# Attention and two feed-forward layers on one core: head 0's decay row, the first zeros, and when two weight conversions run

## The chip, the core and the metric

The kernel runs on one core of a Trainium2 chip. Five engines work side by side, each through its own instructions in order: TensorE (matrix products, PE in the profile), VectorE (DVE), ScalarE (ACT), GpSimd (POOL) and SyncE (SP), which here issues every DMA. The metric is the device time in microseconds, the median over several runs. The order in which each engine gets its instructions is made by a planner when the kernel is built: it takes the program's order as priority and a model of times as its guide, so a line that stands later in the program can come earlier on its engine when its data is there.

## The reference

Three parts follow each other. The first is causal attention with a decay, over 4 batches of 8 heads, 576 positions of 64:

```python
scores = scale * np.matmul(q, k.transpose(0, 1, 3, 2))
cum = np.cumsum(np.maximum(s, 0.0), axis=-1)
bias = -(cum[:, :, :, None] - cum[:, :, None, :])
scores = np.where(causal, -1000000000.0, scores + np.minimum(bias, 0.0))
attn = softmax(scores)
x = attn @ v                      # 2304 tokens x 512 after a transpose
```

The second is `((x @ w1) * (x @ w2)) @ w3 @ w_out` with a width of 1024. The third is `h = x @ w_in`, then `h * softmax(h)`, a layer norm with the gain `g_ln`, and a last product with `w_out`.

## The kernel before

**Attention.** For each head, `qk_part` computes the scores of the causal part in five query tiles (`QT`) as matrix products, `softmax_tile` masks a tile and takes its maximum on VectorE (L195) and its exponential and sum on ScalarE (L199). `normalise` scales the rows by the reciprocal sum on both engines (L227, L228, L235, L237). `tr_part` transposes the probabilities on TensorE (L256) and copies them out of the accumulators (`evict`). `av_parts` multiplies pairs of heads with their values (L284).

The decay is put into the product itself: the operands of a head have 128 rows, 64 with data (64 to 127), and in the lower half a row of ones and a row with the running sum `cum`, the other way round for the keys, and zeros elsewhere. For the first eight heads (`NQ`) these operands stand in plain float32: `QN[h % 3]` and `KN[h % 3]`, three pairs of them. The first two pairs are tiles of their own, the third is `qk3`, which takes over the slot of `s_sb`. Their zeros are memsets, their constant rows come from `const_rows` (ScalarE, L490), and `load_aug` sends the row of `cum` by two small DMAs, row 32 of Q (L155) and row 0 of K (L156). From head 8 on the operands are split into two parts (`split_qk`, with a subtraction on GpSimd at L99 and a copy by DMA at L168).

`cum` is made once: a load of `s`, a scaling (L500) and a scan (L501) on VectorE, and a copy of its last 64 columns to the front (L502). The masks are `wmask`, zero until GpSimd puts the diagonal in after the scan (L517), and `lmask`, a zeroed tile (L499) that then takes two pieces of `wmask`. Before any data is there, TensorE multiplies a zeroed tile with itself eight times (L472).

**The weights.** They arrive as 64-bit floats, 512 KB at a time, in a `stage` tile with two buffers (L394). A conversion (`split_w` with `to_f32`) takes six instructions: ScalarE at L349, VectorE at L355, L356 and L360, then ScalarE (L94) and VectorE (L99) write the two parts of the weight. `pump(n)` in a step loads what fits into the buffers, issues n conversions, each held behind the latest first-tile softmax of a head (`behind`), and loads again. A buffer is free after its conversion.

**Steps.** The loop at L555 runs steps. Step h below 8 computes the scores of head h and transposes head h - 2. Steps 8 and 9 have no scores: they transpose heads 6 and 7 and finish the value products. Step 10 begins with head 8, and from there each step also runs units of `a = x @ w1`, `b = x @ w2` (`ab_unit`, L312; L324 and L332 take them out), as many as `NF` says. `PUMP` says how many conversions a step issues: one each in steps 3, 5 and 6, then two in steps 10 to 15 and one in step 16, sixteen in all for `w1` and `w2`. The units need their weights from step 10 on. After the last head the remaining units, the product of `w3` and `w_out` (L637), the product x (L720), the third part and the output (L854) follow.

The order around the change on SP: the load of `s`, heads 0 and 1, the rows of heads 0 and 1, head 2 (L136, L137) and its row, the two stores of the sums (L513, L516), the gain (L533).

Of the kernel before, what the change touches and what calls it, by code (L numbers as in the profile page):

```python
# [12 lines left out]
AF = mybir.ActivationFunctionType  # L13
# [13 lines left out]
def tile_attention_moe(  # L27
# [15 lines left out]
    nc = tc.nc  # L43
    B, H, D, _, S = qkT.shape
# [7 lines left out]
    HS = S // 2  # L52
# [33 lines left out]
    def smalltile(name):  # L86
        return PSP[1].tile([128, 512], F32, tag="B", name=name)

    def flat(ap):
        return ap.rearrange("p a b -> p (a b)")  # L90
# [25 lines left out]
    lmask = at.tile([128, S], F32, name="lmask")  # L116
# [5 lines left out]
    QN = [t[:, 0] for t in QKN]  # L122
    KN = [t[:, 1] for t in QKN]
# [9 lines left out]
    def load_head(h):  # L133
        b, hh = divmod(h, H)
        if h < NQ:
            nc.sync.dma_start(out=QN[h % 3][64:128], in_=qkT[b, hh, :, 0])  # L136
            after[0] = nc.sync.dma_start(out=KN[h % 3][64:128], in_=qkT[b, hh, :, 1])  # L137
            return
        qk2 = at.tile([128, 2, S], F32, tag="qk2", bufs=2, name="qk2")
        after[0] = nc.sync.dma_start(  # L140
            out=qk2[64:128].rearrange("p a s -> p (a s)"), in_=qkT[b, hh].rearrange("d a s -> d (a s)"),
        )
        raw_t[h] = qk2[64:128]
# [9 lines left out]
    def load_aug(h, src):  # L153
        if h < NQ:
            nc.sync.dma_start(out=QN[h % 3][32:33], in_=src[:, 64:])  # L155
            nc.sync.dma_start(out=KN[h % 3][0:1], in_=src[:, 0:S])  # L156
            return
        nc.sync.dma_start(out=QK[h % 2][32:34, 0].bitcast(F32), in_=src[:, 64:].bitcast(F32))
        nc.sync.dma_start(out=QK[h % 2][0:2, 3].bitcast(F32), in_=src[:, 0:S].bitcast(F32))
# [242 lines left out]
    def pump(n):  # L402
        for _ in range(n):
            load_jobs()
            if loaded:
                raw, conv = loaded.pop(0)

                with ExitStack() as order:
                    for ins in behind:
                        order.enter_context(tc.issue_after(ins))  # L410
                    conv(raw)
        load_jobs()
# [55 lines left out]
    zz = r0.tile([128, HS], F32, tag="a_sb", bufs=2, name="zz")  # L468
    nc.vector.memset(zz, 0.0)
    zp = smalltile("zp")  # L470
    for i in range(8):
        nc.tensor.matmul(zp[:, 0:HS], zz[:, 0:128], zz, start=True, stop=True)  # L472
    s_sb = at.tile([NH, 2, S], F32, tag="qk2", bufs=2, name="s_sb")[:, 0]
    nc.sync.dma_start(out=s_sb, in_=s.rearrange("b h t -> (b h) t"))
# [3 lines left out]
    cum = flat(at.tile([NH, 2, S], F32, tag="qk2", bufs=2, name="cum"))[:, 0:S + 64]  # L478
# [9 lines left out]
    def const_rows(q_, k_):  # L488
        for dst, src, value in ((q_[0:2], zz[0:2], 1.0), (k_[32:34], zz[32:34], -1.0)):
            nc.scalar.activation(  # L490
                out=dst.rearrange("p (a s) -> p a s", a=2), in_=src[:, None, :].broadcast_to((2, 2, HS)),
                func=AF.Copy, scale=0.0, bias=value,
            )

    for i, eng in enumerate((nc.gpsimd, nc.vector)):
        eng.memset(QN[i][0:64], 0.0)
        eng.memset(KN[i][0:64], 0.0)
        const_rows(QN[i], KN[i])
    nc.gpsimd.memset(lmask, 0.0)  # L499
    nc.vector.tensor_scalar(out=s_sb, in0=s_sb, scalar1=0.0, scalar2=1.0 / SCALE, op0=ALU.max, op1=ALU.mult)  # L500
    nc.vector.tensor_tensor_scan(out=cum[:, 64:], data0=s_sb, data1=wmask[0:NH], initial=0.0, op0=ALU.add, op1=ALU.add)  # L501
    nc.vector.tensor_copy(out=cum[:, 0:64], in_=cum[:, S:])  # L502
    for i in range(2):
        load_aug(i, cum[i:i + 1])

    qk3 = at.tile([128, 2, S], F32, tag="qk2", bufs=2, name="qk3")
    QN.append(qk3[:, 0])
    KN.append(qk3[:, 1])
    nc.vector.memset(qk3[0:64], 0.0)
    const_rows(QN[2], KN[2])  # L510
    load_head(2)
    load_aug(2, cum[2:3])
    nc.sync.dma_start(out=cumf_scr, in_=cum)  # L513
    hi(CK[:, 0], cum, nc.vector)
    lo(CK[:, 1], cum, CK[:, 0])
# [2 lines left out]
        out=wmask[:, S - 128:S], in_=wmask[:, S - 128:S], pattern=[[-1, 128]],  # L518
# [5 lines left out]
    behind_scan.__enter__()  # L524
    for st in STAT:
        nc.gpsimd.memset(st, 1.0)
    for t in PT:
        for j in (2, 3, 1):
            nc.gpsimd.memset(t[64:128, KO[j]:KO[j] + 64], 0.0)
    for t in VT:  # L530
        nc.gpsimd.memset(t[0:64, 4], 0.0)
    behind_scan.__exit__(None, None, None)
    nc.sync.dma_start(out=gln, in_=g_ln.rearrange("(k p) -> p k", p=128))  # L533

    for f in range(KF):
# [12 lines left out]
    steps += [(h if h < NH else None, h - 2 if h >= H + 2 else None) for h in range(H, NH + 2)]  # L548
    NF = {10: 3, 11: 0, 12: 3, 13: 0, 14: 3, 15: 2, 16: 2, 17: 0, 18: 1, 19: 1, 20: 1, 21: 2, 22: 2, 23: 2, 24: 2, 25: 2, 26: 2, 27: 2, 28: 2, 29: 2, 30: 2, 31: 2, 32: 2, 33: 2, 34: 3, 35: 3}
    PD, FS = 10, 0.5  # L550
    PUMP = {3: 1, 5: 1, 6: 1, 10: 2, 11: 2, 12: 2, 13: 2, 14: 2, 15: 2, 16: 1}
    PUMP.update((i, 1 if i < 30 else 2) for i in range(22, 34))
    fill = []
    late = []
    for st, (h, ph) in enumerate(steps):  # L555
# [18 lines left out]
        if st > 1:  # L574
            pump(PUMP.get(st, 0))
        if h is not None:
# [461 lines left out]
```

## Time and profile before

| what | value |
|---|---|
| median of 3 runs | 723.62 us (723.31 to 725.47) |
| the profiled execution | 724.28 us, span 722.2 us |
| TensorE busy | 706.0 us (98%) |
| VectorE busy | 509.3 us (71%) |
| ScalarE busy | 467.8 us (65%) |
| GpSimd busy | 94.1 us (13%) |

The span runs from the first instruction to the last; the execution's own time has some 2 us more around it. The shares are means over stages with different limits. Records of TensorE are modelled at their ends, so that its busy share says little in a stretch where it has much waiting; the waits and the busy times of the other engines in that stretch say more. A row of the timeline merges neighbours of one kind: its second number is then the time from the first one's start to the last one's end, with their number behind the x. In brackets stands the engine's idle time before it and what ended it.

### The profile page before, as it was taken

Reading aid. Unit: us, or ns where it says so; the run is one execution under the profiler, and the core shown is the slowest. Engines: PE = TensorE matmul, PEld = TensorE weight load, DVE = VectorE, ACT = ScalarE, POOL = GpSimd, SP = SyncE. Lnnn points to the kernel's source line nnn. Section 1 sums busy time; section 2 is a strip of 40 time slices with the busy share of each in tenths; the row PEclk is TensorE's granted clock in tenths of the full one; section 3 lists DMA queues with packets and bytes.
Section 4 is the critical chain, followed back from the end, with each engine's and each line's share of the span. In section 5 each row is a group of like instructions: output and inputs, shape, how many; then the busy total and the mean of one; then the engine's idle time right before and its main releaser. Section 6 shows DMA issues by size and latency. Waiting matters only on the chain.

```text
span 722.2 us, 12948 instructions
## 1 busy us (share of the span) xinstructions
PE 706.0 (98%) x4642; PEld 630.9 (87%) x4642; DVE 509.3 (71%) x1252; ACT 467.8 (65%) x978; POOL 94.1 (13%) x88
## 2 busy tenths in 40 slices
PE   9989898999999999999999999999999999999998
PEld 6669888889999999999998889988888988888887
DVE  7997989997878888722787985656747366563751
ACT  7997878798866777822544665656647465564742
POOL 2051322143221221000000000001000000000000
PEclk9999999999999999999999999999999999999999
DMA  4654645454476665514565964242334142303211
GB/s 118 191 138 123 175 154 162 154 147 123 138 231 187 193 183 178 183 63 150 181 209 171 331 207 113 66 110 68 82 87 103 44 131 74 89 13 76 59 45 44
DMA packets 79972, 95.53 MB, mean 132 GB/s; under 512 B 41434, under 2 KB 52954, under 8 KB 79908
## 3 DMA queue, kind: packets, MB, share of 16 engines
q1 hardware_dynamic: 79908, 94.71, 45.2%
q8 instruction: 36, 0.59, 0.3%
q14 instruction: 28, 0.23, 0.1%
HBM read 59.04 MB, written 20.17 MB: 110 GB/s over the span
## 4 chain that ended last, share of the span: by engine, by line
PE 76%; DVE 12%; DMA 4%; ACT 4%; issue 2%; POOL 0%; DVEq 0%; ACTq 0%
PE a L312 12%; PE o L854 12%; PE b L312 12%; PE x L720 11%; PE m L637 6%; PE av L284 4%; PE tr L256 4%; PE hX L752 4%; PE hZ L752 3%; DMA turned<-half 3%; DVE P L195 2%; PE sc L186 2%; PE sc L187 2%; ACT P L199 1%; DMA stage<-in_w_dram 1%
## 5 line engine op out<-in xcount | busy, mean ns | idle before, releaser
L199 ACT ACTIVATE P<-P,STAT 128x576 f32<-128x576 f32 (+4 forms) x160 | 88.2, 553 | 18.7 <-DVE STAT L195 18.1
L99 POOL TENSOR_TENSOR QK<-qk,QK 64x1152 fp32r<-64x1152 f32 x24 | 66.6, 2776 | 169.4 <-ACT QK L94 169.3
L720 PE MATMUL x<-gh,ML 128*128 128x256 f32 x288 | 80.3, 279 | 0.0
L720 PE MATMUL x<-gl,MH 128*128 128x256 f32 x288 | 80.1, 279 | 0.0
L720 PE MATMUL x<-gh,MH 128*128 128x256 f32 x288 | 80.0, 279 | 0.0
L312 PE MATMUL a<-xT0h,W 128*128 128x288 f32 x256 | 58.6, 303 | 3.6 <-ACT PT L94 3.3
L312 PE MATMUL b<-xT0h,W 128*128 128x288 f32 x256 | 57.5, 298 | 1.9 <-DVE g_sb L332 1.7
L854 PE MATMUL o<-OH,lh 128*128 128x512 f32 (+1 forms) x152 | 57.7, 379 | 0.2 <-DVE ll L99 0.2
L816 DVE COPY lt<-turned 128x2048 uint16<-128x2048 uint16 x16 | 21.5, 1344 | 51.1 <-DMA turned<-half 51.1
L854 PE MATMUL o<-OL,lh 128*128 128x512 f32 (+1 forms) x152 | 57.5, 378 | 0.0
L854 PE MATMUL o<-OH,ll 128*128 128x512 f32 (+1 forms) x152 | 57.5, 378 | 0.0
L256 PE MATMUL tr<-ident,P 128*128 128x128 f32 x416 | 54.2, 274 | 3.1 <-DVE PT L96 1.0
L312 PE MATMUL a<-xT1h,W 128*128 128x288 f32 x256 | 57.2, 298 | 0.0
L312 PE MATMUL b<-xT1h,W 128*128 128x288 f32 x256 | 56.5, 294 | 0.0
L720 PEld LDWEIGHTS x<-gl,MH 128*128 128x128 f32 x288 | 54.1, 188 | 1.3
L720 PEld LDWEIGHTS x<-gh,MH 128*128 128x128 f32 x288 | 54.1, 188 | 1.0
L720 PEld LDWEIGHTS x<-gh,ML 128*128 128x128 f32 x288 | 54.1, 188 | 0.8
L96 DVE COPY PT<-tr 64x192 f32<-64x192 f32 (+2 forms) x96 | 40.4, 432 | 17.8 <-PE tr L256 17.8
L349 ACT ACTIVATE stage<-stage 128x512 f32<-128x512 f32 x56 | 37.0, 679 | 24.2 <-DMA stage<-in_w_dram 22.0
L256 PEld LDWEIGHTS tr<-ident,P 128*128 128x128 f32 x416 | 47.1, 141 | 5.8 <-DVE PT L96 1.4
L332 DVE TENSOR_TENSOR g_sb<-b,a_sb 128x288 f32<-128x288 f32 x64 | 28.7, 449 | 30.0 <-PE b L312 20.0
L324 ACT ACTIVATE a_sb<-a 128x288 f32<-128x288 f32 x64 | 25.5, 401 | 36.3 <-PE a L312 36.2
(192 smaller groups left out, 1988.0 us busy)
## 6 DMA issues: line engine op xcount, KB each, us to landing
stage<-in_w_dram SPq DMA_DIRECT2D x32, 512.0 KB
g_scr<-g_sb SPq DMA_DIRECT2D x32, 288.0 KB
stage<-in_wo_dram SPq DMA_DIRECT2D x16, 512.0 KB
qk<-in_qk_dram SPq DMA_DIRECT2D x24, 288.0 KB
QK<-QK SPq DMA_DIRECT2D x24, 288.0 KB
gl<-g_scr SPq DMA_DIRECT2D x24, 256.0 KB
wf<-wf_scr SPq DMA_DIRECT2D x22, 256.0 KB
out_dram<-o SPq DMA_DIRECT2D x17, 256.0 KB
```

Of the source, the lines that this page charges most:

```text
L96: eng.tensor_copy(out=dst, in_=src)
L99: last_lo[0] = eng.tensor_tensor(out=dst, in0=src, in1=hi_.bitcast(F32), op=ALU.subtract).ins
L199: ex = nc.scalar.activation(out=dst, in_=dst, func=AF.Exp, bias=st[0:rows, ti:ti + 1], scale=-1.0, accum_out=st[0:rows, 5 + ti:6 + ti],)
L256: last_tr[0] = nc.tensor.transpose(ps[:, 128 * n:128 * n + 128], pt[:, o:o + 128], ident)
L284: nc.tensor.matmul(st["ps"][64 * e:64 * e + 64, 448 + c0:448 + c1], vr[:, j, e], PT[(2 * p + e) % 4][:, o + c0:o + c1], **kw,)
L312: nc.tensor.matmul(ps, w_[:, c, fs], x_[:, c, sl], start=(c == 0 and w_ is WH and x_ is XH), stop=(c == KC - 1 and w_ is WL),)
L332: ab_last[1] = nc.vector.tensor_tensor(out=g[:, sl], in0=ps, in1=st["a"], op=ALU.mult).ins
L349: nc.scalar.activation(out=high.bitcast(F32), in_=high.bitcast(F32), func=AF.Copy, scale=2.0 ** -112)
L637: nc.tensor.matmul(ps, w_[:, k % 4], o_[:, k], start=(k == 0 and w_ is H3 and o_ is WOH), stop=(k == KF - 1 and w_ is L3),)
L720: last = nc.tensor.matmul(ps[:, a], w_[:, k, m * 128:m * 128 + 128], g_[:, k % 2], start=(k == 0 and w_ is MH and g_ is GH), stop=(k == KF ...
L752: last_h[0] = nc.tensor.matmul(ps, x_[:, k], w_[:, k], start=first and k == 0 and x_ is XH and w_ is WH, stop=k == 1 and x_ is XL, skip_gr ...
L854: last = nc.tensor.matmul(ps, l_[:, k], w_[:, k, c0:c1], start=(k == 0 and l_ is LH and w_ is OH), stop=(k == KF - 1 and l_ is LL),)
```

## The change

Head 0's row of `cum` is copied by VectorE instead of sent by two DMAs: the Q row straight behind the scan, the K row behind the copy of the last 64 columns. The eight zero products become four. The zeros of `lmask` are written by ScalarE from the zeroed tile instead of by GpSimd, and the zeros of `qk3` by GpSimd instead of VectorE, at a later place: behind the diagonal and the small memsets of the statistics. The constant rows and the row of head 2 move behind those zeros. Of the three conversions of steps 3, 5 and 6 one stays in step 6; two now stand in steps 8 and 9.

```diff
-    for i in range(8):
+    for i in range(4):
         nc.tensor.matmul(zp[:, 0:HS], zz[:, 0:128], zz, start=True, stop=True)
...
-    nc.gpsimd.memset(lmask, 0.0)
+    nc.scalar.activation(
+        out=lmask.rearrange("p (a s) -> p a s", a=2), in_=zz[:, None, :].broadcast_to((128, 2, HS)), func=AF.Copy,
+    )
     nc.vector.tensor_scalar(out=s_sb, in0=s_sb, scalar1=0.0, scalar2=1.0 / SCALE, op0=ALU.max, op1=ALU.mult)
     nc.vector.tensor_tensor_scan(out=cum[:, 64:], data0=s_sb, data1=wmask[0:NH], initial=0.0, op0=ALU.add, op1=ALU.add)
+    nc.vector.tensor_copy(out=QN[0][32:33], in_=cum[0:1, 64:])
     nc.vector.tensor_copy(out=cum[:, 0:64], in_=cum[:, S:])
-    for i in range(2):
-        load_aug(i, cum[i:i + 1])
+    nc.vector.tensor_copy(out=KN[0][0:1], in_=cum[0:1, 0:S])
+    load_aug(1, cum[1:2])
...
-    nc.vector.memset(qk3[0:64], 0.0)
-    const_rows(QN[2], KN[2])
     load_head(2)
-    load_aug(2, cum[2:3])
...
     for st in STAT:
         nc.gpsimd.memset(st, 1.0)
+    nc.gpsimd.memset(qk3[0:64], 0.0)
...
     behind_scan.__exit__(None, None, None)
+    const_rows(QN[2], KN[2])
+    load_aug(2, cum[2:3])
...
-    PUMP = {3: 1, 5: 1, 6: 1, 10: 2, 11: 2, 12: 2, 13: 2, 14: 2, 15: 2, 16: 1}
+    PUMP = {6: 1, 8: 1, 9: 1, 10: 2, 11: 2, 12: 2, 13: 2, 14: 2, 15: 2, 16: 1}
```

## Rows read from the trace of the kernel before

**Rows 1.** TensorE's waits from 175 us on: total us, times, longest.
```profile
PE hX L752 <- ACT so L758: 0.5, 1, 0.5
```

**Rows 2.** Windows: start:end, length, busy us by engine, clock, DMA share, GB/s.
```profile
10.00:52.00 42.00, 38.09 (x223) 28.69 (x222) 39.41 (x146) 41.90 (x121) 8.49 (x10) 1.00 0.61 165
...
49.00:62.00 13.00, 11.97 (x88) 9.59 (x90) 9.71 (x28) 10.22 (x28) 3.40 (x3) 1.00 0.41 111
```

**Rows 3.** Timeline of the start: start us, us, engine, line, what, [idle before].
```profile
3.75 1.34 DVE L501 TENSOR_TENSOR_SCAN cum<-s_sb,wmask 32x576 f32<-32x576 f32 x1
...
5.12 0.18 DVE L502 COPY cum<-cum 32x64 f32<-32x64 f32 x1
...
5.88 0.53 SPq L156 DMA_DIRECT2D QKN<-cum  x1
...
6.44 0.47 DVE L96 CAST CK<-cum 32x640 fp32r<-32x640 f32 x1
...
9.02 0.76 DVE L195 CUSTOM_DVE_ANT_0 P<-sc,lmask 128x576 f32<-128x576 f32 x1 [1.26 <-PE sc L178]
...
9.82 0.77 ACT L199 ACTIVATE P<-P,STAT 128x576 f32<-128x576 f32 x1 [1.90 <-DVE STAT L195]
```

**Rows 4.** Timeline of TensorE: zero products left at three times, first scores.
```profile
1.25 6.57 PE L472 MATMUL zp<-zz 128*128 128x288 f32 x16 [1.25 <-DVE zz L469]
...
4.29 3.53 PE L472 MATMUL zp<-zz 128*128 128x288 f32 x10
...
6.44 1.38 PE L472 MATMUL zp<-zz 128*128 128x288 f32 x5
...
7.65 0.45 PE L178 MATMUL sc<-QKN 128*128 128x288 f32 x1
```

**Rows 5.** Windows of one us on TensorE: busy us, granted clock.
```profile
118.00:119.00 1.00, 0.00 (x0) 0.91 0.56 129
...
122.00:123.00 1.00, 1.00 (x8) 0.89 0.37 60
```

**Rows 6.** Timeline of the start: what stands around the edits costed at nothing.
```profile
5.49 1.02 DVE L509 MEMSET qk<- 64x1152 f32 x1 [0.19 <-issue]
...
5.50 0.40 ACT L94 ACTIVATE lmask<-wmask 128x64 f32<-128x64 f32 x2 [0.94 <-POOL wmask L517]
...
5.72 1.43 POOL L529 MEMSET PT<- 64x64 f32 x12
...
6.55 1.38 ACT L490 ACTIVATE qk<-zz 2x576 f32<-2x576 f32 x2 [0.65 <-DVE qk L509]
...
9.63 0.59 SPq L156 DMA_DIRECT2D qk<-cum  x1
...
13.15 1.32 PEld L178 LDWEIGHTS sc<-qk 128*128 128x128 f32 x6
```

**Rows 7.** Windows of the staged weights' instructions alone: VectorE's, ScalarE's busy us.
```profile
20.00:36.00 16.00, 4.63 (x8) 2.75 (x4) 1.00 0.65 183
```

**Rows 8.** Timeline of the fifth stage load, step 10's conversions and the next loads.
```profile
48.27 0.36 SPq L394 DMA_DIRECT2D stage<-in_w_dram  x1
...
63.08 1.23 ACT L349 ACTIVATE stage<-stage 128x512 f32<-128x512 f32 x2
...
69.05 0.93 SPq L394 DMA_DIRECT2D stage<-in_w_dram  x2
...
72.56 0.68 ACT L349 ACTIVATE stage<-stage 128x512 f32<-128x512 f32 x1 [0.70 <-DMA stage<-in_w_dram]
```

**Rows 9.** Timeline of two slow conversion operations, GpSimd and TensorE beside them.
```profile
41.57 2.71 POOL L99 TENSOR_TENSOR QK<-qk,QK 64x1152 fp32r<-64x1152 f32 x1
...
42.43 2.42 DVE L360 SCALAR_TENSOR_TENSOR stage<-stage 128x512 uint32<-128x512 uint32 x1
...
114.67 2.83 DVE L360 SCALAR_TENSOR_TENSOR stage<-stage 128x512 uint32<-128x512 uint32 x1
...
119.26 0.58 PE L312 MATMUL a<-xT0h,W 128*128 128x288 f32 x1 [3.34 <-ACT PT L94]
```

## The prediction

> **What bounds the kernel now.** I read the waits of TensorE first, in two halves. After 175 us its longest wait is 0.5 us [rows 1]: from there to the end TensorE sets the pace and is never late. So whatever this change brings must come before that, as an earlier arrival of all engines at the dense part, and the end then moves by as much. All edits lie before 62 us or shift work there.
>
> Then the busy times by stretch. From 10 to 52 us (the eight heads of steps 0 to 7) ScalarE is busy 41.90 of 42.00 us, VectorE 39.41 [rows 2]: ScalarE is the bound, VectorE close behind. From 49 to 62 us (the end of step 7, the two steps without scores, the first head of step 10) they are busy 10.22 and 9.71 of 13.00 us [rows 2], so 2.78 and 3.29 us are free.
>
> Last the start. VectorE's scan ends at 3.75 + 1.34 = 5.09 us; SP issues the second row of head 0 at 5.88; VectorE's first masked maximum stands at 9.02, ScalarE's first exponential at 9.82 [rows 3], and from there ScalarE has no pause. TensorE works off its zero products until 6.44 + 1.38 = 7.82 us and takes up the first scores at 7.65 [rows 4], in its order directly behind them. So two things end together there: the zero products and the row's way through a DMA.
>
> **The start, step by step.** The zero products: 16 records remain at 1.25 us and ten at 4.29, some 490 ns apart (the first a little longer), and the last five take 1.38 us from 6.44, so 240 ns apart and a tail [rows 4]; 480 is the engine at 1.2 GHz, 240 at 2.4. Each product makes two records. Four instead of eight end at about 1.25 + 8 x 0.48 = 5.1 us. They no longer hold the scores.
>
> The row: two copies of 1 x 576 on VectorE replace two DMA issues. Copies there took 0.18 us for 64 columns and 0.47 for 640 [rows 3], so 0.44 for 576. Queue: 5.12 + 0.44 (Q row) + 0.18 (the wrapped 64) + 0.44 (K row) = 6.2, plus 0.1 to TensorE: scores at 6.3 instead of 7.65, **1.35 us earlier**. Bounds: with copies at 0.18 each 1.85; what spoils it stands under the rivals. VectorE's queue behind the copies: today it stood idle for 1.26 us before the first maximum [rows 3], so it was free at 7.76; it loses the 1.02 us memset [rows 6] and gains 0.88, so it is free at 7.62, and the maximum is due at 9.02 - 1.35 = 7.67. That just fits.
>
> Edits that I cost at nothing, with their cover. The zero copy into the mask on ScalarE: some 0.77 us (the 128 x 576 exponential, [rows 3]) in a 0.94 us pause before the two mask pieces [rows 6]; without the pause it delays those by 0.8, and they are due at 7.67, so still nothing. The third head's zeros on GpSimd: some 1.0 to 1.1 us by VectorE's 1.02 for the same [rows 6], after the four small memsets, until about 6.8; its constant rows on ScalarE (1.38 us, [rows 6]) then end near 8.2, and the first exponential is due at 9.82 - 1.35 = 8.47. If the planner puts these zeros behind the twelve memsets of 1.43 us [rows 6], up to 1.2 us of the 1.35 is lost. GpSimd's later memsets move back by 1.1 us and are first read after 18 us. On SP two issues of 0.6 us vanish, so head 1's rows go out 1.27 us earlier; head 2's rows now stand behind both stores of the sums. Before, the second was issued at 9.63 and head 2's scores ran at 13.15 [rows 6], 3.5 us later. SP's queue for it gets shorter by the two issues and longer by the two stores: again about 9.7, for scores at 11.8. Covered, with 2 us.
>
> **The two conversions.** Each is two ScalarE and four VectorE instructions. From 20 to 36 us stand just the two that leave (steps 3 and 5): 2.75 us on ScalarE and 4.63 us on VectorE [rows 7]. The one of step 6 stays in step 6, as the first. As ScalarE is the bound of that stretch, steps 0 to 7 get shorter by **2.75 us**. In steps 8 and 9 the same work must find room: ScalarE's 2.75 in 2.78 free, VectorE's 4.63 in 3.29 free [rows 2], so 1.34 us doesn't fit. Net **1.41 us**. Bounds: 4.63 earlier, if VectorE was the true limit of those steps and the gaps take everything; 1.88 later (2.75 - 4.63), if nothing of VectorE's work fits into gaps because it stands in order ahead of the copies that TensorE's transposes wait for. I take the middle, where the busy times put it.
>
> The loads move too. The stage has two buffers, and each load waits on SP for the conversion that frees its buffer. Now the fifth load is issued at 48.27 and ScalarE takes up step 10's conversions at 63.08 [rows 8], 14.8 us of cover. A load takes 3.5 us from issue to use (69.05 to 72.56, [rows 8]). After the change the fourth load follows step 8's conversion and the fifth step 9's; behind that wait on SP stand the value loads and the copies of split queries and keys of the next heads. I expect the fifth issued near 55 us for a use near 60 and cost it at nothing; the cover falls from 14.8 to about 5 us. The next two loads, issued together at 69.05 today, should then come apart.
>
> **The sum.** 1.35 + 1.41 = 2.76 us. The profiled execution took 724.28 us (span 722.2 and 2.1 around it), 0.66 above the median of 723.62; from the median: **720.9 us**. A difference of 0.3% is 2.2 us, about what a measurement of this kernel can tell from none.
>
> One rule speaks against the start. VectorE's cast of 640 columns took 0.47 us in the midst of GpSimd's run of memsets [rows 3, 6]: memsets didn't hold it. A two-input operation beside GpSimd's 2.71 us subtraction took 2.42 us [rows 9], as one that had to wait. The Trainium skill ("SBUF — State Buffer", on the two separate sides) says that one of the two engines' port pairs is shared and held for a whole instruction, against any GpSimd instruction when VectorE runs in a two-port mode. The second row agrees with it, the first doesn't; by the rule the copies would wait for GpSimd's new memset. What that costs is the third rival.
>
> **Rivals.**
> *The clock stays low, 0.20.* The engine ran its first 4.9 us at 480 ns a record and rose only near 6.2 [rows 4]. In the new order it works until 5.1, rests for 1.2 us and starts the scores at 6.3; nothing in the trace shows whether that is enough. Another slow stretch followed an idle TensorE and lasted from 118.8 to 122.2 us [rows 5], 3.4 us, in which half of the work is done. That costs 1.7: the scores run as if begun at 8.0, 0.35 later than today, and the sum is 1.41 - 0.35 = 1.06: 722.6 us.
> *Step 9's conversion is late, and the load behind it too, 0.15: the slower side.* It stands ahead of the transposes' copies on VectorE, all 4.63 us come on the path (-1.88 in place of +1.41), and the fifth load lands after VectorE and ScalarE, both in order, have reached its conversion. They then stand for up to the 3.5 us of a load. It decides when that conversion ends less than 3.5 us before step 10 takes the next. 723.62 - 1.35 + 1.88 + 3.5 = 727.7 us. For it: the cover shrinks by two thirds. Against: ScalarE comes to step 10's conversions only after five exponentials.
> *GpSimd's memset holds the copies, 0.05.* The K row's copy then ends after the zeros, at about 6.8 + 0.44 in place of 6.2, and 1.0 us of the 1.35 is gone: 721.9 us.
> *The change doesn't move what it says, 0.10.* A planner orders the engines' instructions; the conversions are only held behind head 7's first exponential, and may be drawn into step 7, which is full. Then only one of the two leaves the bound, about 0.7 of the 1.41 is left, or the steps from 10 on, with VectorE's conversions due in each, take up the lead. 721.6 to 723.
> *A later stall vanishes, 0.05.* At 114.67 a conversion's operation took 2.83 us, ScalarE waited, TensorE idled 3.34 us [rows 9] and then lost 1.7 at the low clock. In another order that collision may miss: 5.0 more, 715.9 us. A new one is as easily made.
>
> **Chances and range.** The forecast has 0.45; its own range, with the bounds of copies and gaps weighed, is 718.5 to 722.5, four fifths of it beyond 0.3%. Faster: 0.36 from it, 0.05 from the vanished stall, 0.04 from the others, 0.45. Slower: most of the late load and a little reordering, 0.15. The same: 0.40. The range leaves out the vanished stall, most of the late load and some scatter: 717.6 to 725.6.
>
> **What would show it.** Right at the start: VectorE's first maximum near 7.7, ScalarE's first exponential near 8.5, scores' records 240 ns apart from the first. At 480 the first rival's clock has come. Right in the middle: ScalarE still full until about 48, head 8's scores some 2.8 us earlier than before, no wait for a stage load before 62 us. Wrong: an idle VectorE or ScalarE that ends with a stage load in step 10, or head 8 no earlier than today. And if head 8 is early but the time isn't, the steps from 10 to 16 have taken up the lead.

## The result, and the profile after

The changed kernel took 730.66 us (median of 6 runs, 727.95 to 735.04), the kernel before 724.06 beside it (6 runs, 723.04 to 725.47). The ratio is 1.0099, with a 95% interval of 1.0079 to 1.012: **slower by 1%**. The forecast was 720.9 and faster; 730.66 lies beyond its range and beyond the slow rival's 727.7. The profiled execution took 730.14 us, its span is 728.4.

The distance is complete when head 8 begins. The first score of head 8 stood at 57.51 us before and stands at 64.81 now, 7.30 later; the rest of the span is 664.7 us before and 663.6 after. So the first 65 us hold the answer. Here they are in two stretches, from head 0's first masked maximum to head 7's (steps 0 to 7), and from there to head 8's first score (the end of step 7 and the two steps without scores). First the kernel before, by windows (start:end, length, busy us of PE, PEld, DVE, ACT, POOL, granted clock, DMA share, GB/s):

```profile
9.02:41.79 32.77, 31.27 (x176) 23.65 (x176) 30.78 (x122) 31.92 (x93) 2.44 (x5) 1.00 0.63 173
41.79:57.51 15.72, 13.31 (x97) 10.07 (x93) 13.27 (x37) 14.16 (x39) 7.29 (x6) 1.00 0.55 140
```

and the changed kernel, the same view:

```profile
9.55:42.55 33.00, 31.57 (x165) 23.76 (x164) 26.08 (x110) 29.48 (x88) 0.00 (x0) 1.00 0.47 132
42.55:64.81 22.26, 16.88 (x107) 12.59 (x106) 19.62 (x48) 17.83 (x43) 10.16 (x10) 0.85 0.44 131
```

Two things went against the forecast. The first stretch isn't shorter, although ScalarE has 2.44 us less to do in it and VectorE 4.70 less. And the second is 6.54 us longer, while VectorE's busy time there rose by 6.35, where two conversions are 4.63 [rows 7]: something made its instructions longer.

The start, VectorE's timeline of the changed kernel (start us, us, engine, line, what), which answers to [rows 3]:

```profile
3.22 1.35 DVE L503 TENSOR_TENSOR_SCAN cum<-s_sb,wmask 32x576 f32<-32x576 f32 x1
4.67 0.57 DVE L504 COPY QKN<-cum 1x576 f32<-1x576 f32 x1
5.25 1.11 DVE L505 COPY cum<-cum 32x64 f32<-32x64 f32 x1
6.47 0.53 DVE L506 COPY QKN<-cum 1x576 f32<-1x576 f32 x1
...
9.55 0.76 DVE L195 CUSTOM_DVE_ANT_0 P<-sc,lmask 128x576 f32<-128x576 f32 x1 [1.30 <-PE sc L178]
```

and GpSimd's and TensorE's of the same time:

```profile
5.06 1.26 POOL L527 MEMSET qk<- 64x1152 f32 x1
...
1.24 4.21 PE L472 MATMUL zp<-zz 128*128 128x288 f32 x8 [1.24 <-DVE zz L469]
7.11 8.82 PE L178 MATMUL sc<-QKN 128*128 128x288 f32 x24 [1.65 <-DVE QKN L506]
```

The wrapped copy of 64 columns took 1.11 us where it took 0.18 [rows 3], and ended with GpSimd's new memset (5.25 + 1.11 = 6.36; 5.06 + 1.26 = 6.32). So the scores began at 7.11 instead of the forecast 6.3, and then ran slowly: the records of 128 x 288 at 7.72, 8.20 and 8.68 us stand 480 ns apart, the low level of [rows 4], and those at 13.19, 13.44 and 13.68 stand 240 apart. All of head 0's scores ran at the low clock.

The second stretch: VectorE's instructions of the changed kernel that are longest there, with GpSimd's subtractions for the operands of heads 8 and 9.

```profile
46.42 2.11 DVE L356 SCALAR_TENSOR_TENSOR stage<-stage 128x512 uint32<-128x512 uint32 x1 [0.37 <-ACT stage L349]
...
54.62 2.29 DVE L237 TENSOR_SCALAR P<-P,STAT 64x64 f32<-64x64 f32 x1
...
45.18 2.80 POOL L99 TENSOR_TENSOR QK<-qk,QK 64x1152 fp32r<-64x1152 f32 x1
...
54.23 2.63 POOL L99 TENSOR_TENSOR QK<-qk,QK 64x1152 fp32r<-64x1152 f32 x1 [1.54 <-ACT QK L94]
```

L356 takes 0.68 elsewhere in this stretch, L237 on 64 x 64 takes 0.24. Both now end with GpSimd's instruction or some 0.55 us after it. The chain that ended last, from 46 us to head 8 (start, us, what), shows that this is paid in full:

```profile
46.42 2.11 DVE stage L356
48.53 0.27 DVE PT L96
48.80 0.60 DVE stage L360
...
54.09 0.60 DVE PT L96
54.69 2.22 DVE P L237
56.91 0.33 DVE stage L355
...
57.76 2.18 PE tr L256 x9
59.95 3.34 PE av L284 x22
```

From 46.42 to 57.7 the chain is VectorE alone, instruction after instruction. TensorE, which waited 1.97 and 1.86 us for it, then transposes at the low clock: nine in 2.18 us, where before nine took 1.21. From the end of its last wait it takes 7.05 us to head 8 (57.76 to 64.81) for 22 transposes and 24 value products; before, the same work took 5.82 us (51.69 to 57.51).

### The profile page after: what moved, and what is told of

It reads as the page before. It is cut to its first block, busy times and chain, and to the rows that moved or that the text cites. A ratio compares the mean times of both kernels' runs of the same rounds, so it can differ in the third digit from the quotient of the medians.

```text
span 728.4 us, 12937 instructions
## 1 busy us (share of the span) xinstructions
PE 709.7 (97%) x4634; PEld 633.7 (87%) x4634; DVE 511.1 (70%) x1253; ACT 470.6 (65%) x979; POOL 95.4 (13%) x88
## 4 chain that ended last, share of the span: by engine, by line
PE 85%; DVE 9%; ACT 3%; issue 2%; DMA 2%; DVEq 0%; ACTq 0%
PE x L723 14%; PE o L857 13%; PE a L312 12%; PE b L312 12%; PE m L640 6%; PE av L284 5%; PE hX L755 5%; PE tr L256 5%; PE hZ L755 3%; PE sc L178 2%; DVE P L195 2%; PE sc L186 2%; PE sc L187 2%; PE hW L755 2%; PE hY L755 2%
## 5 line engine op out<-in xcount | busy, mean ns | idle before, releaser
L857 PE MATMUL o<-OH,lh 128*128 128x512 f32 (+1 forms) x152 | 57.7, 379 | 0.2 <-DVE ll L99 0.2
L96 DVE COPY PT<-tr 128x512 f32<-128x512 f32 (+2 forms) x96 | 40.4, 431 | 18.6 <-PE tr L256 18.0
L195 DVE CUSTOM_DVE_ANT_0 P<-sc,wmask 128x448 f32<-128x448 f32 (+3 forms) x128 | 47.3, 412 | 5.2 <-PE sc L178 2.7
```

Source lines behind the costliest of these rows:

```text
L96: eng.tensor_copy(out=dst, in_=src)
L195: mx = nc.vector.tensor_tensor_reduce(out=dst, in0=ps_in, in1=msk, scale=-SCALE, scalar=BIG, op0=ALU.add, op1=ALU.min, accum_out=st[0:rows ...
L857: last = nc.tensor.matmul(ps, l_[:, k], w_[:, k, c0:c1], start=(k == 0 and l_ is LH and w_ is OH), stop=(k == KF - 1 and l_ is LL),)
```

## The experiments

Each run has its own profile; ratios are to the kernel before, timed beside it. In the table "start" is the time of head 0's first maximum, "steps 0-7" and "steps 8-9" are the two stretches above, "rest" is the span after head 8's first score, all in us. These times are of one execution each. In eight of the kernels the start is unchanged, and head 0's first maximum stands anywhere from 8.49 to 9.53 us there: half a microsecond in that column says nothing.

| kernel | ratio (95%) | start | steps 0-7 | steps 8-9 | rest |
|---|---|---|---|---|---|
| before | 1 | 9.02 | 32.77 | 15.72 | 664.7 |
| the change | 1.0099 (1.0079 to 1.012) | 9.55 | 33.00 | 22.26 | 663.6 |
| conversions moved alone | 1.0074 (1.0053 to 1.0095) | 9.02 | 31.18 | 23.07 | 665.2 |
| ... TensorE kept at work | 1.0193 (1.0159 to 1.0226) | 9.02 | 31.16 | 24.14 | 674.1 |
| ... held back longer | 1.004 (1.0028 to 1.0052) | 9.32 | 31.17 | 21.45 | 664.4 |
| ... subtraction in pieces | 0.9988 (0.9975 to 1.0001) | 8.49 | 31.17 | 19.89 | 664.2 |
| one conversion moved | 1.0165 (1.0132 to 1.0199) | 9.13 | 30.23 | 25.04 | 668.7 |
| ... subtraction in pieces | 1.0016 (1.0002 to 1.0029) | 9.53 | 30.23 | 19.54 | 664.5 |
| start alone | 0.9975 (0.9948 to 1.0003) | 9.46 | 33.52 | 15.72 | 662.8 |
| ... eight zero products | 1.0047 (1.0031 to 1.0064) | 9.10 | 35.35 | 15.51 | 665.1 |
| ... zeros in pieces | 0.9961 (0.9945 to 0.9976) | 7.72 | 32.77 | 15.74 | 664.0 |
| before, subtraction in pieces | 0.9968 (0.9951 to 0.9985) | 8.50 | 33.05 | 15.70 | 664.0 |
| the change, both in pieces | 0.9958 (0.9943 to 0.9973) | 7.64 | 31.51 | 19.88 | 660.0 |
| start, both in pieces | 0.9925 (0.991 to 0.994) | 7.64 | 32.82 | 15.68 | 662.1 |

**The two halves of the change, apart.** The conversions moved alone:

```diff
-    PUMP = {3: 1, 5: 1, 6: 1, 10: 2, ...
+    PUMP = {6: 1, 8: 1, 9: 1, 10: 2, ...
```

> The kernel before with the moved conversions alone. After the whole change the first masked maximum of head 7 stood at 42.55 us against 41.79 (0.8 later), the first score of head 8 at 64.81 against 57.51 (7.3 later): 6.5 us were lost in steps 7 to 9, after 1.7 had been made good in steps 1 to 6. If that loss belongs to the moved conversions: head 7's first maximum near 40.0, head 8's first score near 62.3, 4.8 us above the kernel before (some 728.5). If the late start is to blame and the conversions are harmless: head 8's first score near 56, 1 to 2 us below the kernel before (722).

The start alone is the change with the old `PUMP`:

> The changed kernel with the conversions of before (steps 3, 5 and 6). If the start's cost is the 2.4 us by which head 1's first maximum came later (14.23 against 11.79), and nothing absorbs it: 2.4 us above the kernel before, 726. If the late start is what upset steps 7 to 9: 7 us above, 730. If the later stretches absorb it: 723.6.

730.28 and 723.71 us. The moved conversions carry the loss: steps 8-9 grow by 7.35 us and steps 0-7 shrink by only 1.59. The start alone is not slower; its wrapped copy takes the same 1.11 us, and its first scores run at the low clock too, up to 10.8 us.

**Two attempts on the start.** Eight zero products again:

```diff
-    for i in range(4):
+    for i in range(8):
         nc.tensor.matmul(zp[:, 0:HS], zz[:, 0:128], zz, start=True, stop=True)
```

> The second run's kernel with eight zero products again. If the low clock is the start's cost: the scores run at 240 ns a record from 7.6 us on, directly behind the products, head 1's first maximum is at 11.8 as before, the time that of the kernel before within 1 us (723.6). If the start's cost lies in the copies on VectorE or in the later row of head 2: head 1 or head 2 stays 1 to 2 us late and the time at 725 to 726.

and GpSimd's zeros in nine pieces:

```diff
-    nc.gpsimd.memset(qk3[0:64], 0.0)
+    for c in range(9):
+        nc.gpsimd.memset(flat(qk3)[0:64, 128 * c:128 * c + 128], 0.0)
```

> The second run's kernel with the third head's zeros written by GpSimd in nine pieces of 64 x 128 instead of one of 64 x 1152. The copy of 32 x 64 took 1.11 us (0.18 before) beside the one memset of 1.26 us. If VectorE waits for the GpSimd instruction that runs: the copy takes at most 0.4 us, the scores start at 6.2 to 6.4 instead of 7.11. If something else held it (the scan's result, the row behind it): 1.1 us and 7.1 as before. The time, as the clock stays low either way: 0 to 0.8 us below the second run.

The eight products took 728.39 us: head 0 was no earlier than before (9.10), and steps 0-7 took 2.58 us more. Head 1's first maximum is back at 11.87, as expected if the low clock had made it late. But then the heads came in another rhythm (head 3's first maximum at 17.68, head 4's at 27.87; before 17.97 and 24.84), so the planner had made another order, and this run doesn't tell what the products alone are worth. The pieces took 721.74 us, 2.0 below the second run where 0 to 0.8 was expected; the intervals of the two ratios overlap. VectorE, GpSimd and TensorE of that kernel:

```profile
5.37 0.26 DVE L505 COPY cum<-cum 32x64 f32<-32x64 f32 x1
5.73 0.50 DVE L506 COPY QKN<-cum 1x576 f32<-1x576 f32 x1
...
5.18 2.33 POOL L528 MEMSET qk<- 64x128 f32 x9
...
1.24 3.94 PE L472 MATMUL zp<-zz 128*128 128x288 f32 x8 [1.24 <-DVE zz L469]
6.33 5.86 PE L178 MATMUL sc<-QKN 128*128 128x288 f32 x24 [1.15 <-DVE QKN L506]
```

GpSimd needs 2.33 us for the nine where the one took 1.26 (one of them takes 0.90, beside VectorE's row copy and cast), yet the wrapped copy is back at 0.26 us and the scores begin at 6.33, at the full clock. VectorE, ScalarE and TensorE run their instructions in the same order in both kernels, so the earlier scores, 6.33 against 7.02 in the second run, are the pieces' doing. The full clock isn't: it rose at 4.8 us, before the first piece. Head 0 is 1.30 us earlier than before, and head 8 too (56.23 against 57.51).

**Is it TensorE's clock, or the place?** In the kernel with the conversions alone I kept TensorE at work with three products after the transposes of heads 5 and 6:

```diff
                 tr_part(ph, part)
+                if part == 1 and ph in (H - 3, H - 2):
+                    zf = smalltile("zf")
+                    with tc.issue_after(last_tr[0].ins):
+                        for _ in range(3):
+                            nc.tensor.matmul(zf[:, 0:HS], ident, wmask[:, 0:HS], start=True, stop=True)
```

> The first run's kernel (moved conversions alone) with three products of 128 x 288 that nobody reads in each of steps 7 and 8, held behind that step's transposes: 2 x 3 x 0.48 = 2.9 us of work for TensorE in gaps of 1.4, 1.9 and 2.4 us. In the first run the clock was low from 53.2 to 60.0 us; nine transposes took 2.18 us (13 take 1.6 at full clock, so 1.1) and the 24 value products 4.17 (2.92). If the low clock is part of the price: it doesn't fall, head 8's first score comes 2 us earlier than 63.27. If VectorE alone sets the time there: the products fit in, and head 8's first score stays at 63 or comes later. The rest of the order changes too behind 64 us, so the total is a weak sign: 728 against 730.

738.52 us, and head 8 a microsecond later still. The second three products stood behind the wait and not in it (2.33 us before a transpose at 55.37): they ran from 56.19 to 59.17, on the way to head 8. The low stretch was 3.4 us long instead of 6.8, and behind it 22 value products took 2.92 us, where 24 took 4.17 in the first run. So the low clock costs something there, about a microsecond of it seen here, but the products cost more, and no part of the loss is removed by itself. The part after head 8 took 8.9 us more than without them.

**One conversion moved, and two held back longer.**

```diff
-    PUMP = {3: 1, 5: 1, 6: 1, 10: 2, ...
+    PUMP = {3: 1, 6: 1, 8: 1, 10: 2, ...
```

> The kernel before with one conversion moved instead of two: steps 3, 6 and 8. The second half of VectorE's work would then fit into its gaps. If the price grows with the work that doesn't fit: head 8's first score near 58 to 59, the time 724 to 726. If one conversion beside head 7 is enough to bring TensorE's gaps and the low clock: 728 or more. If my estimate was right for half the load: 0.7 us faster than before, 723.

With both moved, and step 8's held until the last tile of head 7, not its first:

```diff
-        if ti == 0:
+        if ti == (3 if h == H - 1 else 0):
             behind[:] = [mx.ins, ex.ins]
```

> The first run's kernel with the conversions of steps 8 and 9 held behind the last maximum and exponential of head 7 instead of its first. In the first run the one of step 8 began on VectorE right behind head 7's first maximum (40.87), among head 7's other tiles. If drawing it into step 7 is the fault: head 7's tiles are done 2 to 3 us earlier, TensorE's gap of 1.9 us goes, head 8's first score near 60, time 727. If VectorE's total is what counts: the work only moves back, 63 and 730, or later, because the second load is freed later.

735.42 us: **one conversion moved costs more than two.** It is nearly as large a move: VectorE has 3.7 us less to do in steps 0-7 (30.78 to 27.09), 1.6 conversions, as the one of step 6 fell behind head 7's first maximum too; and 4.0 us of the loss come after head 8. But the loss doesn't follow the amount of work. Held back longer, two cost 727.16, with head 8 at 61.94, between the two cases expected. What differs in the traces is which instruction of VectorE's stands beside GpSimd's subtraction. The kernel with one moved (VectorE, then GpSimd):

```profile
44.41 3.11 DVE L356 SCALAR_TENSOR_TENSOR stage<-stage 128x512 uint32<-128x512 uint32 x1
51.89 2.88 DVE L99 TENSOR_TENSOR W<-stage,W 128x512 fp32r<-128x512 f32 x1
...
43.70 3.27 POOL L99 TENSOR_TENSOR QK<-qk,QK 64x1152 fp32r<-64x1152 f32 x1 [0.77 <-ACT QK L94]
...
51.60 2.62 POOL L99 TENSOR_TENSOR QK<-qk,QK 64x1152 fp32r<-64x1152 f32 x1
```

In the kernel that held them back longer no instruction of VectorE's took over 1.5 us there, but VectorE then stood idle for 0.72 us for a stage load.

**GpSimd's subtraction in pieces.** The same work and numbers, one instruction of 64 x 1152 as four of 64 x 288:

```diff
-        lo(t[64:128, 1::2], raw, t[64:128, 0::2], G)
+        for a in range(2):
+            for c in (slice(0, HS), slice(HS, S)):
+                lo(t[64:128, 1 + 2 * a, c], raw[:, a, c], t[64:128, 2 * a, c], G)
```

With both conversions moved:

> The first run's kernel with GpSimd's subtraction for the split heads in four pieces of 64 x 288 instead of one of 64 x 1152. In the first run three VectorE operations beside the subtractions and memsets took 2.17, 2.35 and 1.14 us instead of 0.68, 0.24 and 0.54 to 0.6: about 4 us, where the kernel before loses 2.8 (2.42 and 1.21). If that waiting is a main part of the price: no such operation above 1 us, head 8's first score 2 to 3 us earlier than 63.27, the time near 727, and less still since later steps collide too. If VectorE catches up in its gaps: 730.

With one moved:

> Only one conversion moved (steps 3, 6 and 8), with GpSimd's subtraction in four pieces; in one instruction each it took 735.4. If the loss came from VectorE's instructions standing beside GpSimd's long ones, 724 to 728. If the order that the planner makes for this place is the cause, 733 or more.

723.85 us in place of 730.28, and 726.04 in place of 735.42. In both pairs VectorE's and TensorE's instructions stand in the same order up to head 8 (ScalarE's too, but for one copy with both moved), so it isn't another order of the planner's that made the difference. The instructions in question, without and with pieces, both conversions moved. In one piece:

```profile
44.07 2.17 DVE L356 SCALAR_TENSOR_TENSOR stage<-stage 128x512 uint32<-128x512 uint32 x1 [0.31 <-ACT stage L349]
52.27 2.35 DVE L237 TENSOR_SCALAR P<-P,STAT 64x64 f32<-64x64 f32 x1
```

In four (two lines further down in that kernel), with GpSimd's:

```profile
43.53 1.01 DVE L358 SCALAR_TENSOR_TENSOR stage<-stage 128x512 uint32<-128x512 uint32 x1 [0.36 <-ACT stage L351]
51.73 0.30 DVE L239 TENSOR_SCALAR P<-P,STAT 64x64 f32<-64x64 f32 x1
...
42.29 4.12 POOL L99 TENSOR_TENSOR QK<-qk,QK 64x288 fp32r<-64x288 f32 x4
```

The two give back 1.16 + 2.05 = 3.21 us, and the stretches together (steps 0 to 9) shrink by 54.25 - 51.06 = 3.19, though GpSimd itself takes 4.12 us instead of 2.88 (two of its four pieces take 1.26 and 1.24, beside VectorE's operations). That the sums agree to 0.02 us is luck: smaller instructions shifted too (an L237 pair from 1.14 to 1.36, for one), and TensorE's low stretch is 3.4 us long instead of 6.8. The execution in the table took 725.68 us, 1.8 above this kernel's median, so that it rather overstates what is left of the loss. With one moved, steps 8-9 shrink by 5.50; L356 goes from 3.11 to 1.29, no instruction there now takes over 1.3 us, and the granted clock of the stretch rises from 0.86 to 1.00. About half of these 5.50 us is that clock: from its last long wait to head 8 TensorE took 8.95 us in one piece and 5.92 in four, for three transposes (0.3 us) less.

**Does it help everywhere?** The same edit (of the split heads' subtraction, in all three) in the kernel before, in the changed kernel (with the zeros in pieces) and in the one with the new start:

> The kernel before with only GpSimd's part of the subtraction cut into four pieces. If the pauses of VectorE beside GpSimd's subtraction (2.42 and 2.83 us for instructions that take 1.2 to 1.4 alone) are on the path, 721 to 723; if they are not, 724 as before, within 0.5.

> The whole change, with the qk zeros in nine pieces and the subtraction in four. If GpSimd's long instructions are most of what the change loses, the sum of the two parts: 723.9 of the moved conversions with pieces less some 2 us of the start with pieces, 721 to 723. If the moved conversions lose by their place alone, 727 to 730.

> The new start with its zeros in nine pieces, the conversions in steps 3, 5 and 6 as before the change, and GpSimd's part of a conversion's subtraction in four pieces. If GpSimd's long instructions hold VectorE in the old places too, 1 to 3 us below the 721.7 of the run with zeros in pieces, 719 to 721. If the holds there lie beside free time, 721.5 to 722. If the extra instructions of GpSimd make its part end later than VectorE wants it, 722 to 724.

723.0, 722.31 and 719.8 us. (The 1.2 to 1.4 us of the first expectation are two instructions each; one alone takes 0.7.) In the kernel before, the 2.42 us instruction of [rows 9] shrinks to 0.71, and yet steps 0 to 9 stay as long as they were: 48.75 against 48.49, and 48.50 against 48.50 with the new start. Why isn't shown. Other instructions took longer in its stead (L237 on 128 x 192 takes 0.86 us beside a piece, 0.31 alone), so that VectorE's busy time over both stretches fell by only 0.66 us (44.05 to 43.39). What the two kernels gain in these traces lies behind head 8 or in the moment when the clock rises; TensorE's pause of 3.34 us at 119.26 [rows 9], behind a held instruction, is 2.94 and 2.93 us there.

In the changed kernel the pieces take the loss away and turn it into a gain of 0.4%. Head 8 still comes 1.52 us later than before (59.03); the gain lies behind it. Its windows:

```profile
7.64:39.15 31.51, 29.86 (x165) 22.75 (x164) 26.14 (x110) 29.90 (x89) 1.29 (x14) 1.00 0.55 145
39.15:59.03 19.88, 16.29 (x108) 11.88 (x106) 17.96 (x48) 17.23 (x43) 12.68 (x16) 0.91 0.53 148
```

VectorE's busy time in the second stretch is 17.96 us, the 13.27 of before and 4.69, about the 4.63 of two conversions. The stretch is still 4.16 us longer than before. The start with both kinds of pieces and the conversions left where they were is the fastest kernel here, 0.9925 (0.991 to 0.994).

## Why the prediction was wrong

**That everything is decided before the dense part: right.** A delay of 7.30 us at head 8 changed the rest of the span by only 1.1. It is no constant, though: in the other kernels the rest moved by -4.7 to +9.4 us.

**The start, 1.35 us: right in its working, wrong in one decision.** I weighed GpSimd's memset against VectorE's copies and decided by the cast that took 0.47 us "in the midst of GpSimd's run of memsets". I misread that row. Ten of these twelve memsets take 0.15 us each; the two that began while the cast ran (6.44 to 6.91) took 0.50 and 0.47:

```profile
6.50 0.56 POOL L529 MEMSET PT<- 64x64 f32 x2
```

The cast wasn't held because it had begun first; GpSimd was. In the new order GpSimd's memset of 1.26 us began first, and the copy took 1.11. The third rival was the right one, at 0.05; by its working 1.0 us would go, and the scores came 0.8 later than forecast. The rule that the prediction named and set aside (the Trainium skill, "SBUF — State Buffer", on the two separate sides: a shared port pair is held for a whole instruction) agrees with every row shown here; that pieces shorten the wait is what it would lead one to expect. With the zeros in pieces head 0 came 1.30 us earlier, near the 1.35, in an execution whose clock was up in time.

Head 1 came 2.44 us late because head 0's scores ran at the low clock, as the first rival had it. The moment when the clock rises differs from one execution to the next: the same sixteen zero records took 6.57 us in the kernel before, 5.74 and 7.13 in two kernels with an unchanged start. In the nine traces with eight zero products it rises between 4.3 and 7.3 us, always before the scores; in the five with four products at 4.2, 4.8, 4.8, 10.8 and 13.1. Four products at the low clock end at 5.45 us, and in six of the nine the rise came later than that. So leaving out four products seems to be what exposes the scores, in some executions; no run has shown it by itself, as the one with eight products had another order.

**Steps 0 to 7, 2.75 us shorter: mis-sized.** The step was "as ScalarE is the bound of that stretch". Moved alone, ScalarE lost 2.63 us of work (31.92 to 29.29 busy) but the stretch only 1.59. With one conversion moved it lost 2.95, the stretch 2.54. And it was partly the fourth rival: in the changed kernel step 8's first operation stands at 43.23, right behind head 7's first maximum, so it was drawn into step 7.

**Steps 8 and 9: this is the step that failed.** I put "VectorE's 4.63 in 3.29 free" and let 1.34 us remain. With the conversions moved alone the stretch grew by 7.35 us, and with the subtraction in pieces still by 4.17. It can be split where TensorE's last wait for VectorE ends:

| kernel | from head 7's first maximum to there | from there to head 8 |
|---|---|---|
| before | 9.90 | 5.82 |
| conversions moved alone | 15.27 | 7.80 |
| ... subtraction in pieces | 11.60 | 8.29, for seven transposes more |

TensorE's rows, of the kernel before, of the conversions moved alone and of the pieces:

```profile
51.69 1.21 PE L256 MATMUL tr<-ident,P 128*128 128x128 f32 x9 [0.79 <-DVE PT L96]
...
55.47 2.18 PE L256 MATMUL tr<-ident,P 128*128 128x128 f32 x9 [2.41 <-DVE PT L96]
57.58 4.17 PE L284 MATMUL av<-PT,VT 128*64 128x64 f32 x24
...
51.26 3.12 PE L258 MATMUL tr<-ident,P 128*128 128x128 f32 x16 [2.12 <-DVE STAT L197]
54.31 3.72 PE L286 MATMUL av<-PT,VT 128*64 128x64 f32 x24
```

The free time was an average over a window that reached to 62 us, beyond head 8's first score at 57.51, and it says nothing of where the pauses lie. VectorE's two pauses of before in this stretch:

```profile
50.95 0.97 DVE L96 COPY PT<-tr 128x512 f32<-128x512 f32 x2 [0.48 <-PE tr L256]
...
56.48 0.69 DVE L96 COPY PT<-tr 128x512 f32<-128x512 f32 x1 [1.72 <-PE tr L256]
```

Only the first, 0.48 us, lies ahead of TensorE's last wait. Both are waits for transposes, and the transposes wait for VectorE's copies: work put ahead of a copy delays the transpose and pushes the next pause along. The second lies behind the last wait, where TensorE has 5.82 us of its own left. In the run with pieces step 9's whole conversion, 2.9 us on VectorE, stands there and delays nothing up to head 8; step 8's stands ahead, and TensorE's last wait ends 1.70 us later. With the seven transposes that wait with it (0.76 us) 2.46 us came on the path even with the subtraction in pieces, where I had 1.34. The other 1.7 us of the 4.17 are the low clock, a term I had left out here.

The bound that I named, "if nothing of VectorE's work fits into gaps", came near the measured sum, 1.88 against -1.60 + 4.17 = 2.57 us later (31.17 and 19.89 against 32.77 and 15.72), but by luck: part of the work did fit, and the clock made up for it.

**A term that was missing: 3.19 us.** I had the row of a conversion's operation held beside GpSimd's subtraction [rows 9] and used it as a chance for a gain at 114 us, with "a new one is as easily made" behind it. I didn't ask what stands beside the two subtractions for heads 8 and 9, which run just in the stretch that I was filling. In the new place the pieces give back 3.19 us with both moved, in the old place nothing. With the holds the moved conversions cost 54.25 - 48.49 = 5.76 us up to head 8, where I had a gain of 1.41.

**The slow rival** had the right sign by a mechanism of which one half held (VectorE's work on the path). The other half didn't: between 39 and 62 us no wait for a stage load stands on VectorE, ScalarE or TensorE, and in the 37 us behind head 8 ScalarE and VectorE wait 2.8 and 2.0 us for stage loads, where before it was 2.8 and 2.2. The fourth and fifth load were issued at 53.43 and 62.72, later than the 55 that I expected for the fifth, and the next two still together, at 76.42, where I had them come apart.

**What stays open.** TensorE's low clock is part of the price: on the way to head 8 it cost 1.2 us in the changed kernel (7.05 against 5.82), 2.0 with the conversions moved alone, 1.7 of what the pieces left. In these three kernels the low stretch began within a wait for VectorE of about 2 us or up to 1.3 us after one. But such a wait doesn't settle it: in the run with one conversion moved and the subtraction in pieces TensorE waited 2.10 us, and steps 8 and 9 have the full clock. No run removed the low clock alone, as the attempt with extra products failed. In the changed kernel the pieces also shorten the part after head 8 by 3.6 us (663.6 to 660.0). The changed kernel has a 2.83 us L360 at 121.83 as before, a 3.34 us pause of TensorE behind it and then 6.8 us of low clock; with the pieces the pause is 1.66 us and no low stretch follows. The pause and the clock would make more than 3.6 us together, and in the run held back longer no low stretch followed a pause of 3.34 us either, so how much of this is the pieces' doing isn't shown.

## What to carry to other kernels

Before moving work into "free" time of an engine, look whether the pauses are waits on a partner that in turn waits for this engine. Only the time behind the partner's last wait is room; ahead of it pauses move along, and the busy share overstates them. When moving VectorE's work, list what GpSimd runs in the new place: an instruction may be held there until GpSimd's ends. What a hold costs depends on the place; the same pieces gave 3.19 us in one and nothing in another. Where holds can't be avoided, cut GpSimd's instruction into pieces, even if GpSimd itself gets slower. And when a row seems to show that an engine isn't held, look at the other engine's instructions one by one: a mean over twelve hid the two that waited.

## What was not expected of the hardware

- A copy of 32 x 64, 0.18 us before, took 1.11 us beside one memset of 1.26 us, and 0.26 beside a ninth of it. GpSimd waits likewise where VectorE began first: 0.50 us for a memset that takes 0.15.
- Cutting GpSimd's subtraction in four made GpSimd slower (4.12 against 2.88 us in the same place) and the kernel before faster: 0.9968 (0.9951 to 0.9985).
- Moving one conversion cost 11.0 us against before, moving two 5.3, with the same instructions; with the subtraction in pieces one costs 0.9 us and two gain 0.5, each against the kernel before beside it.
